# A fused mLSTM cell and gated feed-forward: the head of the kernel is put in another order, and some of its work on other engines

## The chip, the cores and the metric

The kernel runs on one core of a Trainium2 chip. [...] PEld is PE's loading of weights. The metric is the device time of one execution in microseconds.

## The reference

```python
for t in range(S):                      # B=4, H=8, S=768, D=40
    m_new = np.maximum(f_gate[:, :, t] + m, i_gate[:, :, t])
    f_stab = np.exp(f_gate[:, :, t] + m - m_new)
    i_stab = np.exp(i_gate[:, :, t] - m_new)
    m = m_new
    C = f_stab[..., None, None] * C + i_stab[..., None, None] * np.einsum('bhd,bhe->bhde', vt, kt)
    n = f_stab[:, :, None] * n + i_stab[:, :, None] * kt
    h_tilde = np.einsum('bhde,bhe->bhd', C, qt)
    denom = np.maximum(np.abs(np.einsum('bhd,bhd->bh', n, qt)[:, :, None]), 1.0)
    y[:, :, t] = h_tilde / denom / (1.0 + np.exp(-o_gate[:, :, t]))
x = y.transpose(0, 2, 1, 3).reshape(B * S, H * D)     # 3072 x 320
h = x @ w_in                                          # w_in 320 x 2048
out = (h * np.cos(h)) @ w_out                         # w_out 2048 x 320
```

The inputs are fp32; the weights `w_in` and `w_out` are given in fp64.

## The kernel before, in words

The sequence is cut into 6 chunks of 128 steps. One chunk of one batch is a *cell*: 24 cells, n = 0 to 23, 8 heads each. In a cell the recurrence becomes an attention with a decay matrix E (128 x 8 x 128 entries): E comes from the running maxima of the gates, spread over all partitions, less a column of its own (`decay_exponents`), with the upper part cut off by an affine select on GpSimd, and an exponential on ACT (`decay`). Then `turn` (transposes of q and k on PE) and `turn_out` (copies to SBUF), `scores` (q times k), `weigh` (times E), `values` (times v), `normalize` (by the denominators and the sigmoid of `o_gate`, giving y), `seam` (PE turns y into x's layout and makes the state's increment), `seam_out` and `state` (copies from PSUM). For the four cells of the first chunk the state is empty; from cell 4 on (called cell B in the prediction) a carried state is added, and cells are treated in another layout.

When the four cells of a chunk are done, the feed-forward for its 512 tokens can start: 8 pairs of 128-wide blocks of d_ff, each pair an `Up` (products with `w_in` into two PSUM banks, eviction on ACT at `near`, L723, then DVE and ACT make h cos h) and a `down` (products with `w_out`). The next chunk's cells run in between, so the order is: the four cells of chunk 0 (the *head*, `first_cells`, L1063), then for each chunk its feed-forward with the next chunk's cells.

The fp64 weights come as pairs of 32-bit words and are put together on the chip, piece by piece: `take_apart` (two ACT instructions), `bound` (two on DVE), `join` (one on DVE), `round_up` (an integer addition on GpSimd, L187). `weights_in(f)` is three pieces: two of 128x512 and `w_in_l` of 128x256. The raw words land in one of four quarters of the tile `blocks`, used in turn; cell 3's E takes a quarter too.

The order on every engine is written by hand: the program is traced under `tc.manual_schedule()`, and each engine runs its instructions in the order in which the Python code makes them. The code of the head sets it. All loads are issued by SP in one queue, in the code's order; a load that has to wait holds up all behind it. An issue also waits for the load eight places ahead of it.

What the change and the prediction touch:

- Fillings: constant tiles are filled by GpSimd (L101 to L131, L232 to L234) and DVE (L94 to L99, L125) before the head begins.
- `gates_first` (L246): scan, subtraction and scan on DVE for the first chunk's gates; the maxima M0 (32 rows, one for each batch and head) go to DRAM by a DMA of GpSimd (L252), from where they are spread over 128 partitions by a load (`load_M`, L406, 512 KB a cell). For cells in `SPREAD` PE spreads them instead (`spread`, L419: products with a column of the identity repeated 128 times).
- `gates_sums`, `gates_less_sums`, `gates_maxima`, `gates_exponents`, `gates_exp`, `gates_turn`, `gates_diagonal`: the same for the five later chunks, 32 rows of 640. `gates_maxima` ends with a GpSimd DMA to DRAM (L278), which cell B's E is loaded from (L404); `gates_exp` ends with two (L291), which G (L500) is loaded from.
- `warm(k)`: k products of zeros on PE, whose result nobody reads.
- PSUM banks: `psum(n)` gives even cells of the head one pool of two banks and odd ones another of four; the pool of the `Up` has two.

Of the kernel before, what the change touches and what calls it, by code (L numbers as in the profile page):

```python
# [11 lines left out]
FP = mybir.dt.float32  # L12
# [17 lines left out]
def kernel(  # L30
# [33 lines left out]
    NK = DM // 128  # L64
    KL = NK * 128
    assert DM - KL == 64 and NF % 2 == 0
    SPREAD = (0, 1)

    const = ctx.enter_context(tc.tile_pool(name="const", bufs=1))
    wp = ctx.enter_context(tc.tile_pool(name="wp", bufs=1))  # L70
# [9 lines left out]
    ps_o = ctx.enter_context(tc.tile_pool(name="ps_o", bufs=4, space=bass.MemoryType.PSUM))  # L80


    ident = const.tile([128, 128], FP, name="ident")
    make_identity(nc, ident)
    room = const.tile([128, 3, NF // 2, 128], FP, name="room")
    small = room[:, 2].rearrange("p k n -> p (k n)")
    wall = small[:, 0:256].bitcast(BF).rearrange("p (h t) -> p h t", t=C)
    ident_b = small[:, 256:320].bitcast(BF)
    nil = small[:, 320:384].bitcast(BF)
    yo = small[:, 384:384 + DM]  # L90
    blocks = const.tile([128, 40, C], FP, name="blocks")
    S_AT, S_RING, D_AT, D_RING, FREE_AT = 0, 3, 12, 10, 32
    one = const.tile([BH, 1], FP, name="one")
# [1 line left out]
    least = const.tile([128, H], FP, name="least")  # L95
    nc.vector.memset(least, TWO_PI)
    firsts = blocks[:, 32:36]
    M0_all = firsts[:, 2]
    nc.vector.memset(M0_all, 0.0)  # L99

    nc.gpsimd.memset(wall, 0.0)  # L101
    nc.gpsimd.affine_select(out=wall, in_=wall, compare_op=OP.is_ge, fill=1.0e30, base=0,
# [2 lines left out]

    DV = 48
    ks_wide = room[:, 0:2].rearrange("p i k n -> p (i k n)").rearrange("p (b h d) -> p b h d", b=B, h=H)
    nc.gpsimd.memset(ks_wide[:, :, :, D:64], 0.0)
    ks2 = [const.tile([128, 2, H, D], FP, name=f"ks{i}") for i in range(2)]
    vs2 = [const.tile([128, 2, H, DV], FP, name=f"vs{i}") for i in range(2)]  # L110
    for i in range(2):
        nc.gpsimd.memset(vs2[i][:, :, :, D:DV], 1.0)

    vr2 = [const.tile([128, 2, HP, 3, 8, 2], FP, name=f"vr{i}") for i in range(2)]
    for t in vr2:
        nc.gpsimd.memset(t, 1.0)
        nc.gpsimd.memset(t[:, :, :, 1], 0.0)

    WR = HP * (C // 32) * D
    raws = {w: [const.tile([128, WR + 32], FP, name=f"{w}r{i}") for i in range(2)] for w in "qk"}
    for i in range(2):
        for w in "qk":
            nc.vector.memset(raws[w][i], 0.0)  # L125

    st = [const.tile([128, 2 * HP * DV], FP, name=f"st{b}") for b in range(B)]
    for t in st:
        nc.gpsimd.memset(t, 0.0)
    og = const.tile([128, B, 3 * C // 32, 32], FP, name="og")  # L130
    nc.gpsimd.memset(og, 0.0)  # L131

    w_in_sb = wp.tile([128, NK, DFF], FP, name="w_in_sb")

# [94 lines left out]
    a1, F1, M1, keep, shift = (t.rearrange("r (c s) -> r c s", c=R) for t in spare)  # L229
    m0 = gates.tile([BH, R], FP, name="m0")  # L230
    dd = gates.tile([BH, R - 1, BH], FP, name="dd")
    nc.gpsimd.memset(keep, 1.0)  # L232
    nc.gpsimd.memset(keep[:, :, 0:1], 0.0)
    nc.gpsimd.memset(shift, 0.0)  # L234

    fg, ig = (g.rearrange("b h s -> (b h) s") for g in (f_gate, i_gate))

# [8 lines left out]
    def gates_first():  # L246
# [6 lines left out]
        nc.vector.tensor_scalar(out=nM, in0=M0[:, C - 1:C], scalar1=-1.0, scalar2=None, op0=OP.mult)  # L253
        nc.scalar.activation(out=e0, in_=a0, func=AF.Exp, bias=nM)

    def gates_first_out():
        pg = ps_o.tile([128, 2, BH], FP, name="pg", tag="o")
        for j, src in enumerate((a0, e0)):
            nc.tensor.transpose(pg[:, j], src, ident[0:BH, 0:BH])
        nc.vector.tensor_copy(out=tab[:, 0, 0:2], in_=pg)  # L260
# [7 lines left out]
        nc.vector.tensor_tensor_scan(out=flat[0], data0=flat[3], data1=flat[0], initial=0.0, op0=OP.mult, op1=OP.add)  # L268

    def gates_less_sums():  # L270
        nc.vector.tensor_tensor(out=a1, in0=a1, in1=F1, op=OP.subtract)
        nc.vector.tensor_copy(out=shift[:, 0, 0:1], in_=F0[:, last])
        nc.vector.tensor_copy(out=shift[:, 1:R, 0:1], in_=F1[:, 0:R - 1, last])

    def gates_maxima():
        nc.vector.tensor_tensor_scan(out=flat[1], data0=flat[4], data1=flat[2], initial=M0[:, last],
# [106 lines left out]
    def load_E(n):  # L383
        load_M(n)
        if n >= B and n % 2 == 0:
            load_G(n)
# [28 lines left out]
    def spread(n, i):  # L415

        for p in range(HP):
            g = n * H + HP * i + p
            nc.tensor.matmul(pm[n, i][:, p], ident[:, g:g + 1].to_broadcast([128, 128]), M0_all,  # L419
                             start=False, stop=(p == HP - 1))  # L420

    def psum_o():
# [2 lines left out]
    def cols(n, j, width):  # L425
        c, b = divmod(n, B)
        return tab[:, c, j, ts(b, H)].unsqueeze(2).to_broadcast([128, H, width])


    def decay_exponents(n):  # L430
        E = Es[n]
        if n < B:
            nc.vector.tensor_tensor(out=E, in0=E, in1=cols(n, 0, C), op=OP.subtract)
        nc.gpsimd.affine_select(out=E, in_=E, compare_op=OP.is_ge, fill=1.0e30, base=0,  # L434
                                pattern=[[0, H], [1, C]], channel_multiplier=-1)

# [24 lines left out]
    def psum(n):  # L461

        return (ps_o, "o") if n < B and n % 2 == 1 else (ps_a, "a")
# [187 lines left out]

    def seam(n):

        pool, tag = psum(n)
        if n < B:
            px = pool.tile([128, NK + 1, C], FP, name="px", tag=tag)
            for i in range(NK):
                nc.tensor.transpose(px[:, i], ys[n][:, ts(i, 128)], ident)
            for e in range(2):
                nc.tensor.matmul(px[64 * e:64 * e + 64, NK], ys[n][:, KL:DM], ident, start=True, stop=True)  # L660
            pxs[n] = px
        if n < N - B:
            pu = pool.tile([128, HP, DV], FP, name="pu", tag=tag)
            for p in range(HP):
                for j in range(2):
                    h = 2 * p + j
                    nc.tensor.matmul(pu[64 * j:64 * j + D, p], kws[n][:, h], vs(n)[:, h], start=True, stop=True)  # L667
            pus[n] = pu
# [389 lines left out]
    def warm(k, bank=None):  # L1058

        for _ in range(k):  # L1060
            nc.tensor.matmul(bank or pw, nil, nil.unsqueeze(1).to_broadcast([128, HP, 128]), start=True, stop=True)

    def first_cells():  # L1063
        nc.vector.memset(nil, 0.0)
        gates_in()
        nc.scalar.copy(out=ident_b, in_=ident)
        load(0, "qk")
        later_gates_in()
        load(0, "v")
        load(1, "qk")  # L1070
        load_o(0, (0, 1))
        load(1, "v")
        load(2, "qk")
        load_E(0)
        load_E(1)
        warm(12)
        wall_in(0, 0, pmu)
        wall_in(0, 1, psum_o())
        gates_first()
        gates_first_out()  # L1080
        spread(0, 0)
        decay_exponents_half(0, 0)
        turn(0)
        turn_out(0, False)
        gates_sums()
        spread(0, 1)
        decay_exponents_half(0, 1)
        decay(0)
        weigh_k(0)
        load_E(2)  # L1090
        load(2, "v")
        load_E(3)
        load_o(0, (2, 3))
        load(3)
        first = weights_in(0)
        pieces.extend(next(first) for _ in range(NK))
        wall_in(1, 0, psum_o())
        wall_in(1, 1, psum_o())
        gates_less_sums()
        spread(1, 0)  # L1100
        decay_exponents_half(1, 0)
        scores(0)
        gates_maxima()
        turn(1)
        weigh(0)
        sigmoid(0, slice(0, 2))
        turn_out(1, False)
        spread(1, 1)
        decay_exponents_half(1, 1)
        gates_exponents()  # L1110
        decay(1)
        weigh_k(1)
        values(0)
        load_M(B)
        pieces.extend(first)
        load_blocks(B)
        normalize(0)
        scores(1)
        gates_exp()
        load_G_of(B)  # L1120
        turn(2)
        turn_out(2, False)
        gates_turn()
        seam(0)
        load(B, "kv")
        outs.append((0, weights_out(0)))
        load_blocks(B + 1)
        weigh(1)
        seam_out(0)
        state(0)  # L1130
        decay_exponents(2)
        gates_diagonal()
        decay(2)
        weigh_k(2)
        values(1)
        normalize(1)
        scores(2)
        turn(3)
        sigmoid(0, slice(2, 4))
        seam(1)  # L1140
        weigh(2)
        decay_exponents(3)
        turn_out(3)
        seam_out(1)
        values(2)
        decay(3)
        weigh_k(3)
        state(1)
        normalize(2)
        scores(3)  # L1150
        warm(2)
        seam(2)
        weigh(3)
        to_float32(*pieces.pop(0))
        seam_out(2)
        state(2)
        for piece in pieces[0:2]:
            take_apart(*piece)
        values(3)
        pd = gates_spread()  # L1160
        warm(6)
        more = weights_in(1)
        pieces.extend(next(more) for _ in range(NK))
        load_M(B + 1)
        normalize(3)
        bound(pieces[0][0])
        put_together(*pieces.pop(0))
        seam(3)
        seam_out(3)
        decay_exponents(B)  # L1170
        bound(pieces[0][0])
        put_together(*pieces.pop(0))
        gates_keep(pd)
        pieces.extend(more)
        load_G_of(B + 1)
        load(B + 1, "kv")
        outs.append((1, weights_out(1)))
        load_o(1)
        outs.append((2, weights_out(2)))
        low_dimensions(B)  # L1180
        turn_blocks(B)
        state(3)
        decay(B)
        scale_q(B)
        weigh_k(B)
        odd_values_of(B)

    spot = const.tile([1, 1], FP, name="spot")
    nc.gpsimd.memset(spot, 0.0)

    def sin_next():

# [320 lines left out]
```

## Time and profile before

| what | us |
|---|---|
| median of 3 runs | 514.96 (514.72 to 515.9) |
| the profiled execution | 515.31 |
| its span (first to last instruction) | 513.5 |
| PE busy in the span | 498.9 (97%) |
| DVE, ACT, POOL busy | 418.5, 326.4, 301.9 |
| first `values` of cell 0, 1, 2, 3 (PE, L546) | 17.59, 23.89, 28.84, 33.42 |
| first product of the first `Up` (L715) | 38.44 |
| first eviction of the first `Up` (ACT, L723) | 43.77 |

The profile is of one execution. Its rows give a start, a duration, the engine, the line of the kernel, the operation and `out<-in`; in brackets stands how long the engine idled ahead of the row and what ended that. Times in rows are counted from the first instruction.

### The profile page before, as it was taken

What the parts mean: (1) busy time and instruction counts of PE and PEld (TensorE: products, weight loads), DVE (VectorE), ACT (ScalarE), POOL (GpSimd) and SP (SyncE); (2) the same over time, 40 slices, a digit from 0 to 9 for tenths busy, and PEclk for the clock granted to TensorE, in tenths of its full rate; (3) what the DMA queues carried; (4) which work ended last, traced back from release to release, by engine and by line L of the source; (5) the groups of instructions that cost most, each with busy time, mean ns of one, the idle gap of its engine ahead of it and who ended that gap; (6) DMA issues with size and microseconds to landing.
All of it is one profiled execution on the core that took longest, in us unless ns stands there. A gap on an engine that the chain in (4) does not pass through costs nothing.

```text
span 513.5 us, 11097 instructions
## 1 busy us (share of the span) xinstructions
PE 498.9 (97%) x4038; PEld 377.0 (73%) x4038; DVE 418.5 (82%) x839; ACT 326.4 (64%) x618; POOL 301.9 (59%) x387
## 2 busy tenths in 40 slices
PE   6999998999999999999999999999999999999997
PEld 3874554655676677778878778878778878687876
DVE  4889998987788888789988979988979867677655
ACT  2889887686944647748658757658857654443541
POOL 7525656543924955857576868566767455535340
PEclk9999999999999999999999999999999999999999
DMA  9989999899066527306829105928202000010001
GB/s 136 212 187 251 263 194 248 194 257 182 32 173 138 129 73 139 94 32 175 180 65 179 55 31 157 186 76 172 61 32 80 5 5 6 2 52 0 1 0 54
DMA packets 100903, 57.87 MB, mean 113 GB/s; under 512 B 63520, under 2 KB 93312, under 8 KB 100848
## 3 DMA queue, kind: packets, MB, share of 16 engines
q1 hardware_dynamic: 97696, 55.48, 46.3%
q10 hardware_dynamic: 2752, 1.23, 0.9%
q8 instruction: 32, 0.52, 0.5%
q0 software_dynamic: 400, 0.44, 0.3%
q14 instruction: 23, 0.19, 0.1%
HBM read 51.71 MB, written 4.11 MB: 109 GB/s over the span
## 4 chain that ended last, share of the span: by engine, by line
PE 71%; DVE 5%; ACT 5%; DMA 3%; POOL 2%; issue 2%; SPq 1%; ACTq 0%; DVEq 0%; POOLq 0%
PE acc L979 23%; PE pup L783 16%; PE pup L715 7%; PE pup L799 6%; PE late L979 4%; PE po L829 3%; PE ps L530 3%; PE pup L709 2%; PE vt L565 2%; PE vt L556 2%; DVE t L508 1%; DMA bits<-in_moe_w_out_dram 1%; PE pu L667 1%; DMA E<-M_d 1%; ACT E L448 1%
## 5 line engine op out<-in xcount | busy, mean ns | idle before, releaser
L723 ACT ACTIVATE n<-pup 128x512 int32<-128x512 f32 x64 | 36.9, 593 | 96.4 <-DVE pup L808 64.9
L731 ACT ACTIVATE n<-n 128x512 f32<-128x512 f32 x96 | 58.2, 627 | 21.1 <-DVE n L726 15.6
L818 POOL TENSOR_TENSOR g<-g,n 128x512 f32<-128x512 f32 x31 | 39.5, 1275 | 50.9 <-ACT n L731 46.8
L715 PE MATMUL pup<-xT,w_in_sb 128*128 128x512 f32 x128 | 58.8, 602 | 1.9 <-DVE g L735 1.7
L726 DVE SCALAR_TENSOR_TENSOR n<-pup,n 128x512 f32<-128x512 f32 x64 | 43.1, 688 | 21.3 <-ACT n L723 18.8
L979 PE MATMUL acc<-w_out_sb,g 128*128 128x160 f32 x320 | 58.4, 302 | 0.0
L800 POOL TENSOR_TENSOR blocks<-blocks 128x256 f32<-128x256 f32 x32 | 25.6, 801 | 53.3 <-ACT blocks L792 53.2
L979 PE MATMUL acc<-T,g 128*128 128x160 f32 x304 | 55.8, 301 | 0.0
L783 PE MATMUL pup<-xT,w_in_sb 128*128 128x256 f32 x192 | 53.0, 385 | 0.4 <-ACT blocks L792 0.2
L448 ACT ACTIVATE E<-E,tab 128x128 f32<-128x128 f32 x160 | 50.2, 391 | 3.3 <-POOL E L434 3.1
L979 PEld LDWEIGHTS acc<-w_out_sb,g 128*128 128x128 f32 x320 | 48.9, 190 | 4.5 <-issue 2.7
L735 DVE TENSOR_TENSOR g<-pup,n 128x512 f32<-128x512 f32 x64 | 42.6, 687 | 6.0 <-ACT n L731 5.6
L715 PEld LDWEIGHTS pup<-xT,w_in_sb 128*128 128x128 f32 x128 | 23.0, 189 | 33.0 <-issue 31.1
L979 PEld LDWEIGHTS acc<-T,g 128*128 128x128 f32 x304 | 46.0, 190 | 0.9 <-issue 0.4
L783 PEld LDWEIGHTS pup<-xT,w_in_sb 128*128 128x128 f32 x192 | 33.8, 189 | 9.6 <-ACT blocks L792 5.8
L808 DVE TENSOR_TENSOR pup<-pup,blocks 128x256 f32<-128x256 f32 x32 | 13.9, 436 | 30.6 <-PE pup L799 27.3
L783 PE MATMUL pup<-x_room,room 128*128 128x256 f32 x128 | 38.2, 380 | 0.0
L791 ACT COPY blocks<-pup 128x512 f32<-128x512 f32 x32 | 18.6, 580 | 29.8 <-PE pup L783 27.9
L829 PE MATMUL po<-w_out_sb,g 128*128 128x320 f32 x128 | 36.3, 436 | 0.8 <-POOL w_out_sb L187 0.7
L979 PE MATMUL acc<-T,blocks 128*128 128x160 f32 x160 | 36.2, 308 | 0.0
L799 PE MATMUL pup<-xL,w_in_l 64*128 64x512 f32 x128 | 36.1, 641 | 0.0
L512 POOL TENSOR_TENSOR qG<-t,G 128x512 f32<-128x512 f32 x20 | 25.9, 1293 | 17.1 <-DVE t L508 16.8
(214 smaller groups left out, 1221.9 us busy)
## 6 DMA issues: line engine op xcount, KB each, us to landing
E<-M_d SPq DMA_DIRECT2D x21, 512.0 KB
qr<-in_q_dram SPq DMA_DIRECT2D x72, 80.0 KB
kr<-in_k_dram SPq DMA_DIRECT2D x72, 80.0 KB
bits<-in_moe_w_out_dram SPq DMA_DIRECT2D x8, 640.0 KB
G<-G_d SPq DMA_DIRECT2D x18, 256.0 KB
blocks<-in_moe_w_in_dram SPq DMA_DIRECT2D x32, 128.0 KB
out_dram<-o_sb SPq DMA_DIRECT2D x23, 160.0 KB
o<-in_o_gate_dram SPq DMA_DIRECT2D x40, 80.0 KB
```

Source lines behind the costliest of these rows:

```text
L448: nc.scalar.activation(out=Es[n][:, h], in_=Es[n][:, h], func=AF.Exp, scale=-1.0, bias=tab[:, c, 0, g:g + 1])
L512: nc.gpsimd.tensor_tensor(out=qG, in0=qkT[n][0], in1=Gs[n], op=OP.mult)
L715: nc.tensor.matmul(pu.rearrange("p (b t) -> p b t", b=B), w_in_sb[:, i, ts(2 * f2 + e, 128)], xT[c][:, i:NK * B:NK], start=(i == 0 and not ...
L723: nc.scalar.activation(out=self.n[e], in_=self.pu[e], func=AF.Copy, bias=0.25)
L726: nc.vector.scalar_tensor_tensor(out=self.n[e].bitcast(FP), in0=self.pu[e], scalar=0.25, in1=self.n[e], op0=OP.add, op1=OP.subtract)
L731: nc.scalar.activation(out=r, in_=r, func=AF.Sin, scale=TWO_PI_DOWN)
L735: nc.vector.tensor_tensor(out=g, in0=self.pu[e], in1=self.n[e].bitcast(FP), op=OP.mult)
L783: nc.tensor.matmul(bank[:, part].rearrange("p (b t) -> p b t", b=B // 2), w[:, f2], x, start=start, stop=stop, skip_group_check=True)
L799: nc.tensor.matmul(pu, w_in_l[r, f2], xL[c][r].rearrange("p b t -> p (b t)"), start=False, stop=True, skip_group_check=True)
L818: tt(out=self.g, in0=self.g, in1=self.n[e].bitcast(FP), op=OP.mult)
L829: nc.tensor.matmul(po[c][b], gs[c, f][:, ts(b, C)], w_out_sb[:, f], start=(f == 0), stop=(f == NF - 1))
L979: nc.tensor.matmul(a, lhs, rhs, start=start, stop=stop)
```

## The change

The head is put in another order, and some of its work moves to other engines.

- Fillings are done on other engines and at other times: `nil` (zeros for `warm`) first; `ks_wide` on DVE; `raws`, `st`, `vr2` on GpSimd inside the head; only the part of `og` that no load overwrites is zeroed.
- `SPREAD` takes cell 2 in: its E is no longer loaded. The maxima are split into three bf16 parts that add up to the fp32 value (`maxima_in_parts`), stacked in 96 rows of `M0_parts`, and `spread` multiplies them by three stacked identities (`of_parts`) in bf16.
- Loads: cell 3's E and v, q, k follow the second chunk of loads directly, then the first `w_in` pieces, all three ahead of cell B's E.
- `gates_less_sums` and the subtraction of cell 3's E (`decay_exponents`) move from DVE to GpSimd.
- `seam` of the even cells uses the banks of the `Up`.
- `warm` is 9 at the start instead of 12, `warm(2)` goes, `warm(6)` uses another bank. `exp_next` loads ACT's exponential table early.
- The later gates' maxima, exponents and turn come later; the first piece's `put_together` comes after `normalize(3)`.

```diff
-    SPREAD = (0, 1)
+    SPREAD = (0, 1, 2)
...
-    nc.gpsimd.memset(ks_wide[:, :, :, D:64], 0.0)
+    nc.vector.memset(ks_wide[:, :, :, D:64], 0.0)
...
+    def blocks_constants():
+        for i in range(2):
+            for w in "qk":
+                nc.gpsimd.memset(raws[w][i], 0.0)
...
+    def odd_constants():
+        for t in vr2:
+            nc.gpsimd.memset(t, 1.0)
+            nc.gpsimd.memset(t[:, :, :, 1], 0.0)
...
+    def maxima_in_parts():
+
+        rest, mid = blocks[0:BH, 36], blocks[0:BH, 37].bitcast(BF)[:, 0:C]
+        hi = M0_parts[0:BH]
+        nc.vector.tensor_copy(out=hi, in_=M0)
+        nc.vector.tensor_tensor(out=rest, in0=M0, in1=hi, op=OP.subtract)
+        nc.vector.tensor_copy(out=mid, in_=rest)
+        nc.vector.tensor_tensor(out=rest, in0=rest, in1=mid, op=OP.subtract)
+        nc.vector.tensor_copy(out=M0_parts[2 * BH:3 * BH], in_=rest)
+        nc.scalar.copy(out=M0_parts[BH:2 * BH], in_=mid)
...
     def gates_less_sums():
-        nc.vector.tensor_tensor(out=a1, in0=a1, in1=F1, op=OP.subtract)
+        nc.gpsimd.tensor_tensor(out=a1, in0=a1, in1=F1, op=OP.subtract)
...
-            nc.tensor.matmul(pm[n, i][:, p], ident[:, g:g + 1].to_broadcast([128, 128]), M0_all,
+            nc.tensor.matmul(pm[n, i][:, p], of_parts[:, g:g + 1].to_broadcast([128, 128]), M0_parts,
                              start=False, stop=(p == HP - 1))
...
         if n < B:
-            nc.vector.tensor_tensor(out=E, in0=E, in1=cols(n, 0, C), op=OP.subtract)
+            nc.gpsimd.tensor_tensor(out=E, in0=E, in1=cols(n, 0, C), op=OP.subtract)
...
-        pool, tag = psum(n)
+        pool, tag = (ps_u, "up") if n < B and n % 2 == 0 else psum(n)
...
+    def decay_in(n):
+        for i in range(2):
+            wall_in(n, i, pmu if (n, i) == (0, 0) else psum_o())
+        for i in range(2):
+            spread(n, i)
+        for i in range(2):
+            decay_exponents_half(n, i)
```

The end of the new `first_cells`, from cell 2's scores on:

```python
        scores(2)
        weigh(2)
        weigh_k(2)
        seam(1)
        seam_out(1)
        state(1)
        turn(3)
        turn_out(3, False)
        gates_maxima()
        gates_exponents()
        load_M(B)
        load_blocks(B)
        load(B, "kv")
        outs.append((0, weights_out(0)))
        load_blocks(B + 1)
        values(2)
        decay(3)
        sigmoid(0, slice(2, 4))
        scores(3)
        normalize(2)
        weigh(3)
        seam(2)
        weigh_k(3)
        values(3)
        gates_exp()
        load_G_of(B)
        gates_diagonal()
        gates_turn()
        for piece in pieces[0:1]:
            take_apart(*piece)
        bound(pieces[0][0])
        seam_out(2)
        state(2)
        for piece in pieces[1:2]:
            take_apart(*piece)
        pd = gates_spread()
        warm(6, psum_o())
        normalize(3)
        put_together(*pieces.pop(0))
        more = weights_in(1)
        pieces.extend(next(more) for _ in range(NK))
        load_M(B + 1)
        seam(3)
        seam_out(3)
```

## The prediction

> **What bounds the kernel now.** I read the page's tenths first. From the third of the 40 slices on PE is at 9, and from 128 us PE is the whole story. The edits touch only the first 45 us; from the first up projection on, every engine's instructions stand in the old order. So the question is how much earlier or later that projection is reached, and what of the difference survives until PE takes over. The table by stretches shows the head and what follows it (busy us of each engine, granted clock, DMA share, GB/s):
>
> ```profile
> 10.00:20.00 10.00, 9.84 (x93) 9.16 (x94) 7.92 (x14) 6.95 (x9) 3.44 (x6) 1.00 1.10 214
> 20.00:30.00 10.00, 9.71 (x125) 8.66 (x123) 8.17 (x18) 8.98 (x19) 4.64 (x7) 1.00 0.94 205
> 30.00:40.00 10.00, 9.78 (x98) 6.82 (x97) 8.95 (x24) 8.63 (x26) 4.19 (x4) 1.00 0.78 184
> ...
> 44.00:60.00 16.00, 16.00 (x128) 9.02 (x125) 15.20 (x30) 13.46 (x25) 6.65 (x9) 1.00 1.00 242
> 60.00:95.00 35.00, 32.27 (x258) 19.08 (x258) 31.75 (x61) 29.95 (x58) 21.28 (x25) 1.00 0.91 222
> ```
>
> Up to 95 us two things are full: the DMA engines, and from 44 us DVE (15.20 of 16). Nothing there can catch up; a head that ends later leaves its lateness to DVE, and a load that starts later leaves it to the DMAs. The chain of waits shows the one place where they meet:
>
> ```profile
> 50.34 5.67 DMA bits<-in_moe_w_out_dram
> ...
> 56.03 3.38 DMA o<-in_o_gate_dram
> ...
> 59.46 1.28 ACT L352
> ```
>
> There ACT waited 0.68 us for a DMA: compute has 0.68 us to spare against the queue. Next the head's end, by engine and time:
>
> ```profile
> 35.37 1.30 POOL L187 TENSOR_TENSOR w_in_sb<-w_in_sb,blocks 128x512 int32<-128x512 int32 x1 [3.73 <-ACT st L690]
> 38.75 1.41 POOL L187 TENSOR_TENSOR w_in_sb<-w_in_sb,blocks 128x512 int32<-128x512 int32 x1 [2.08 <-DMA vs<-in_v_dram]
> 40.12 1.14 POOL L434 TENSOR_SCALAR_AFFINE_SELECT E<-E 128x1024 f32<-128x1024 f32 x1
> 41.68 0.74 POOL L187 TENSOR_TENSOR w_in_l<-w_in_l,blocks 128x256 int32<-128x256 int32 x1 [0.41 <-issue]
> ```
>
> ```profile
> 38.73 0.28 DVE L173 TENSOR_SCALAR w_in_l<-w_in_l 128x256 f32<-128x256 f32 x1
> 39.05 1.26 DVE L174 TENSOR_SCALAR w_in_l<-w_in_l 128x256 int32<-128x256 int32 x1
> 40.35 1.19 DVE L183 SCALAR_TENSOR_TENSOR w_in_l<-blocks,w_in_l 128x256 int32<-128x256 int32 x1
> ```
>
> The first up projection starts at 38.44, its last products wait for GpSimd's 41.68 row, and its first eviction starts at 43.77 (call this N). Two DVE rows of 0.3 to 0.4 us took 1.26 and 1.19: each ended only as a GpSimd row beside it did. DVE and GpSimd hold each other up when both work on SBUF alone. Rows that read PSUM don't show it (the 128x512 subtraction at 18.06 took 0.67 beside a GpSimd row of 1.26).
>
> ```profile
> M_d<-w_out_sb POOLq DMA_DIRECT2D x1, 80.0 KB, 5.5
> ```
>
> The later maxima reach DRAM 5.5 us after their issue at 17.26; their first load, of cell B's E, is issued at 26.56 and doesn't wait.
>
> **The change, part by part.** Times are the trace's clock; one execution, 515.31 us, a span of 513.5 and 1.8 around it, 0.35 above the median 514.96.
>
> *Fillings.* DVE's four 0.62 us fillings (L125) leave ahead of the gates' scan and 0.72 of `ks_wide` comes (0.74 on GpSimd), with two small ones: the scan starts at about 2.35 instead of 3.88 (the gate's packets end at 2.07). `nil` is filled first, so the warming products start at 1.0 instead of 4.02; nine at 0.425 end at 4.9.
>
> *Maxima in parts.* Five DVE rows of 0.14 to 0.30 (as L253, L249) take 1.1: parts at 4.75, hidden by the warming products. The trace has no such spread in bf16. Below, a bf16 product and its weight load take 0.11 (L1061 at 31.84); above, the fp32 pair takes 0.24. I take 0.11 to 0.13, four in 0.45 against 0.97.
>
> *Early cells.* From there: halves of E at 6.6 (11.37 before), exponential 9.1 (14.06), scores 9.2 (14.35), values of cell 0 at 11.2 (17.59), of cell 1 at 15.5 (23.89). This lead of 6 to 8 us is what the change buys; the rest asks what remains of it.
>
> *DMA.* One broadcast of E (512 KB; 2.5 us at 205 to 214 GB/s) disappears, so cell 3's q, k and v land about 2 us earlier. The fp32 subtraction on DVE (1.21) goes with it.
>
> *Subtraction of cell 3 on GpSimd.* 128x512 takes 1.28 there (L512), so 128x1024 about 2.5. E of cell 3 lands at about 16.2, so it runs 16.2 to 18.7, then the select, 1.1. DVE wants the SBUF-only product of `normalize(0)` at 17.9 and that of `normalize(1)` at 19.4. By the 39.05 row they wait for the GpSimd row at hand: y of cell 0 at 20.4 instead of 18.4, of cell 1 at 22.0 instead of 19.9. Queued behind them on DVE: `weigh(2)` and the scan of the maxima (1.53), which ends at 25.2 (23.6 without the hold-up).
>
> *Late maxima.* They are now written at 25.2, against 17.26. At 5.5 us they land at about 30.5. SP stands at E of cell B, and behind it the blocks, k, v, w_out and the next w_in. Without the wait SP would be there at 26.56 − 2.5 + 2.7 (four w_in_l issues, 26.95 to 29.66, now ahead of it) = 26.8. So 3.7 us are lost to a gain of 2.5; but the 2.1 us that SP waited on E at 31.1 go as well. Net: the queue is between 0.9 us early and 1 us late; I take 0.3 late.
>
> *Sigmoid and exponents.* The second sigmoid moves behind cell 3's exponential on ACT (table load 1.28, 0.74): it ends at 28.5 (26.9 without hold-up) and `normalize(2)` waits for it; y of cell 2 at 30.1, `weigh(3)` to 31.3, values of cell 3 31 to 33. That is 2.4 of the lead left (33.42 before).
>
> *The turn of the gates.* Its ten transposes (0.8) stand on PE behind values of cell 3, its copy (0.41) on ACT ahead of `take_apart` of the first piece (0.67), and on DVE `bound` of that piece (0.92) ahead of `normalize(3)` (1.6): 33.0 + 0.8 + 0.4 + 0.7 + 0.9 + 1.6 = 37.4 for y of cell 3, against 37.09. The lead is gone; without the hold-up it is 35.5.
>
> *Behind y.* Before, GpSimd rounded the first piece at 35.37, under `normalize(3)`. Now `join` (0.69) and rounding (1.30) follow y, so GpSimd has 1.30, 1.14, 1.41 and 0.74 in a row, with DVE's 0.92, 0.69, 0.64 and 0.45 in between, each in the other's way. GpSimd alone: 37.4 + 0.7 + 0.1 + 4.6 = 42.8, low products to 43.9, N at 44.0. With each in turn waiting for the other (0.92 + 0.69 + 0.64 + 0.45 added): N at 46.7. Before, 0.4 of such waiting showed up in GpSimd's rows; I take 60% of the way, N = 45.6.
>
> *Filler for odd values.* 1.1 us on GpSimd ahead of a copy at 44.53, which PE reads at 47.29: 2.5 us of cover, then nothing. *Seams in other banks, sums of the gates, exp_next (1.28 of table load at 14.4):* under the lead, nothing. If the lead were gone by then, the load would cost its 1.28.
>
> Sum: N 1.8 late, of which 0.68 is absorbed where ACT waited: +1.1 us. 515.31 + 1.1 = 516.4, by the median 516.1, so +0.2%. 0.2% (1.0 us) is also about what a measurement here can tell from no change.
>
> [...] The row says 5.5 us for these 80 KB, and the sum stands on it. [...]
>
> **Rivals.**
> *A. Faster.* GpSimd's subtraction doesn't hold DVE up. Place: `normalize(0)` at 17.9. It decides when cell 3's E lands 2.5 us later, after y of cell 1, or when DVE's product goes through beside it. Then y of cell 3 is at 35.5, N at 43.0 (cell B's eight exponentials on ACT end then) to 43.8, the maxima land at 29. Queue and compute are 0.8 to 2.5 early: 512.5 to 514.2, say 513.8. For it: 18.06 went undisturbed, cells lead by 8 us at 16 us. Against it: the y product at 20.61 took 1.09 beside a GpSimd row instead of 0.56.
> *B. Nothing.* N is at most 1.2 late and the 0.68 covers most: 515.0. For it: before, the held-up rows cost GpSimd only 0.4.
> *C. Cold PE.* `warm(2)` is gone, and by my times PE stands from 26.4 to 29.9. Products run at half speed after a pause here: 12 took 5.10 us at the start, 6 took 1.47 at 35.75. Place: values of cell 3 and the transposes, 2.8 us, doubled: 518.9 at the worst. [...]
> [...]
> *D. Queue.* The maxima take 7 us (bigger packets of w_in beside them): E of cell B at 32, everything behind it 1.8 late, and the wait on `o` with it: 516.8.
>
> **How the numbers follow.** Forecast 0.40 (0.33 over 0.2%, 0.07 within), A 0.36 (0.32 faster, 0.04 within), B 0.12 (within), C 0.06 and D 0.06 (slower). Faster 0.32, same 0.23, slower 0.45. The range reaches from A's 512.6 to C's 518.5. The forecast's own is 515.2 (N at 44.5) to 517.6 (46.7 and a late queue).
>
> **What would show it.** Values of cell 0 at about 11 and of cell 1 at 15 to 16; the GpSimd subtraction of about 2.5 us, and the y product beside it longer than 0.56; SP idle 2 to 4 us ahead of cell B's E; ACT waiting for the turned gates and DVE for the first Abs; N after 43.8. Wrong if N is before 43.5, or if E of cell B is issued before 27.

## The result, and the profile after

In the rows PE is TensorE, DVE VectorE, ACT ScalarE and POOL GpSimd; SP is SyncE, which here only issues DMAs. The changed kernel takes 518.73 us (median of five, 517.76 to 518.93); the kernel before, on the same chip, 514.72 (513.95 to 515.9). The ratio is 1.0074, 95% interval 1.0055 to 1.0092: slower by 0.74%, and just above the predicted range. The profiled execution took 518.73, with a span of 516.9 (before 513.5).

| start, us | before | after |
|---|---|---|
| values of cell 0 | 17.59 | 10.61 |
| values of cell 1 | 23.89 | 14.50 |
| values of cell 2 | 28.84 | 22.59 |
| values of cell 3 (and how long they took) | 33.42 (1.98) | 30.20 (3.64) |
| y of cell 3, end | 37.09 | 38.44 |
| first product of the first `Up` | 38.44 | 40.52 |
| first eviction of the first `Up` (N) | 43.77 | 47.32 |

The cells start up to 9.4 us earlier, keep 3.2 of it as far as the values of cell 3, and have lost it all 8 us later. N is 3.55 later and the span 3.4 longer: next to nothing of the lateness was absorbed. The page of after shows in its tenths what was not there before, in the row of the granted clock: the third slice (25.8 to 38.8 us) has 5, half speed.

```profile
span 516.9 us, 11081 instructions
...
PE   9978998999999999999999999999999999999997
...
PEclk9959999999999999999999999999999999999999
```

A fine table of the clock puts the fall at 26.87 and the rise at 40.53: 13.65 us. Here is the table by stretches of 3.41 us, a quarter of that, around it (busy us of PE, PEld, DVE, ACT, POOL, then granted clock, DMA share, GB/s):

```profile
23.46:26.87 3.41, 2.10 (x26) 1.86 (x24) 0.74 (x5) 3.36 (x5) 2.99 (x5) 1.00 0.93 236
26.87:30.28 3.41, 1.97 (x23) 1.52 (x23) 2.88 (x6) 2.51 (x3) 2.21 (x4) 0.50 0.49 138
30.28:33.70 3.42, 3.42 (x16) 3.41 (x16) 0.00 (x0) 0.00 (x0) 0.00 (x0) 0.50 1.12 262
33.70:37.11 3.41, 3.41 (x17) 2.14 (x17) 0.95 (x4) 2.04 (x7) 0.00 (x0) 0.50 0.94 266
37.11:40.52 3.41, 3.12 (x26) 1.59 (x24) 2.19 (x8) 2.55 (x9) 1.34 (x2) 0.50 1.07 248
40.52:43.93 3.41, 1.98 (x4) 0.67 (x4) 3.31 (x5) 3.25 (x13) 2.27 (x2) 1.00 0.80 220
```

From 30.28 to 33.70 PE works alone, at half speed, while DVE, ACT and GpSimd stand: the chain runs through PE's cold products. The rows of that stretch, PE first, then who waits:

```profile
28.32 0.69 PE L680 MATMUL px<-ident,y 128*128 128x128 f32 x2 [2.75 <-DVE y L646]
...
30.20 3.64 PE L568 MATMUL ph<-vs,blocks 128*128 128x41 f32 x16
33.77 1.27 PE L324 MATMUL pg<-ident,w_out_sb 32*128 32x32 f32 x10
```

```profile
35.08 0.43 ACT L325 COPY tab<-pg 128x320 f32<-128x320 f32 x1 [5.68 <-PE pg L324]
```

```profile
36.09 0.43 DVE L182 TENSOR_SCALAR w_in_sb<-w_in_sb 128x512 f32<-128x512 f32 x1 [6.30 <-ACT w_in_sb L176]
```

PE had stood for 2.75 us ahead of the transposes of cell 2, waiting for y (in the kernel before, `warm(2)` stood there). ACT waits 5.68 for the turn of the gates, DVE 6.30 for the first piece, and only then comes `normalize(3)`, and after it N:

```profile
47.32 1.09 ACT L745 ACTIVATE n<-pup 128x512 int32<-128x512 f32 x2 [1.82 <-PE pup L731]
```

This is rival C, to which the prediction gave 0.06.

### The profile page after: what moved, and what is told of

Its sections match the earlier page's. It is cut to its first block, busy times and chain, and to the rows that moved or that the text cites. A ratio compares the mean times of both kernels' runs of the same rounds, so it can differ in the third digit from the quotient of the medians.

```text
span 516.9 us, 11081 instructions
## 1 busy us (share of the span) xinstructions
PE 500.5 (97%) x4027; PEld 377.8 (73%) x4027; DVE 417.3 (81%) x838; ACT 327.7 (63%) x624; POOL 305.6 (59%) x393
## 4 chain that ended last, share of the span: by engine, by line
PE 67%; DMA 10%; DVE 7%; SPq 5%; issue 4%; POOL 4%; ACT 3%; DVEq 0%; POOLq 0%; ACTq 0%
PE acc L1001 21%; PE pup L805 15%; PE pup L737 6%; PE pup L821 6%; PE late L1001 4%; PE ps L552 3%; DMA G<-G_d 3%; PE po L851 3%; DMA bits<-in_moe_w_out_dram 2%; DMA qr<-in_q_dram 2%; PE pup L731 2%; DMA blocks<-in_moe_w_in_dram 2%; PE vt L587 2%; PE vt L578 1%; DVE n L748 1%
```

## The experiments

Times are medians; the ratio is to the kernel before on the same chip. "Wide products" are those of `warm`: 128x512 in bf16, of zeros, whose result nobody reads. "With the clock up" means: over the executions alone whose mean granted clock is 0.998 or more, as 3.41 us at half speed, the shortest fall in the traces of the head, takes 0.0033 off the mean (3.41 x 0.5 / 515). N is read in the profiled execution.

### Wide products in PE's pause, and the subtraction back on DVE

Theories: *the clock*; *the hold-up* of DVE's y product by GpSimd's subtraction; *the queue*, that is, the late maxima that SP waits for.

```diff
         weigh(3)
+        warm(10, psum_o())
         seam(2)
```

> The changed kernel with ten empty bf16 products on PE ahead of the transposes of cell 2, where PE stood from 25.6 to 28.3 us. They need 2.2 us, and the y they would otherwise wait for ends at 28.4. The clock theory (the granted clock fell at 26.9 because PE stood, and stayed at 0.50 until 40.5): the clock stays at 1.00; the values of cell 3 take 2.0 us instead of 3.64, the turn of the gates 0.75 instead of 1.27, and y of cell 3 ends at 36.1 instead of 38.44; the first eviction of the first up projection (47.32) comes at 44.5 to 45.0, the time at 515.7 to 516.5 us. The queue theory (the late maxima stand in SP's way, and the loads behind them set the pace): values of cell 3 faster all the same, but the first eviction at 46.5 or later and the time at 517.8 or more. The hold-up theory (GpSimd's subtraction costs DVE about 2 us, the clock the rest): 517.0 to 517.5.

516.43 us, ratio 1.0028 (1.0013 to 1.0042); N 45.01.

```profile
28.92 1.98 PE L568 MATMUL ph<-vs,blocks 128*128 128x41 f32 x16
...
35.05 0.41 PE L680 MATMUL px<-ident,y 128*128 128x128 f32 x2 [1.72 <-DVE y L646]
...
37.12 6.80 PE L737 MATMUL pup<-xT,w_in_sb 128*128 128x512 f32 x8 [0.95 <-POOL w_in_sb L196]
```

The values of cell 3 are back at 1.98, and more than half of the loss is gone, as the clock theory said. But the clock still falls, later: PE stood 1.72 us ahead of cell 3's transposes, the clock was at half speed from 36.31 to 43.13, and the first `Up` took 6.80 us, where it had taken 3.75 in the kernel before.

```diff
-            nc.gpsimd.tensor_tensor(out=E, in0=E, in1=cols(n, 0, C), op=OP.subtract)
+            nc.vector.tensor_tensor(out=E, in0=E, in1=cols(n, 0, C), op=OP.subtract)
```

> The changed kernel with cell 3's subtraction on DVE again (128x1024 in 1.2 us) instead of GpSimd (1.90 us). Hold-up theory: y of cell 1 ends 1.5 to 2 us earlier than 20.9, everything behind it as well, and the time is 516.5 to 517.2. Clock theory: y of cell 1 ends at 20.3, 0.6 earlier, because DVE now does the subtraction itself; PE still stands for more than 2 us before the transposes of cell 2, the clock falls again, and the time is 517.8 to 518.7.

518.69, ratio 1.0053 (1.0036 to 1.0070); N 47.30, against 47.32. PE stood 2.75 us again and the clock fell for 10.24 us. The place of the subtraction alone is worth nothing that shows: what GpSimd cost DVE by the hold-up, DVE now pays by doing it.

Both edits together:

> The changed kernel with both edits: the ten empty products in PE's pause and cell 3's subtraction on DVE. Clock theory: what the products alone give (515.7 to 516.5), less 0.3 to 0.7. Hold-up theory: 514.5 to 515.2, as the two costs add up. Queue theory: 517.5 or more.

516.40, ratio 1.0015 (1.0002 to 1.0028); N 45.51, the first `Up` cold again (6.88). The two costs don't add up: the hold-up theory, in the size that the prediction gave it, falls. The 0.3 to 0.7 us that the clock theory expected below the products alone (516.43) didn't come either.

### The kernel before without its two products

```diff
-        warm(2)
         seam(2)
```

> The kernel before without the two empty products ahead of cell 2's transposes (31.84 us). If the fall of the clock comes from the pause and not from the two products that are missing, nothing changes: PE stands for 0.5 us there at most, the clock stays at 1.00, and the time is 514.2 to 515.2. If the two products alone kept the clock up, the clock falls to 0.50 for a stretch between 32 and 45 us, and the time is 516.5 to 518.5.

515.25, ratio 0.9999 (0.9986 to 1.0012); PE stands 0.42 us there and the clock stays at 1.00. Two products missing are nothing in the old order. It is the new order that makes a pause of 2.75 us in their place: the second sigmoid, which y of cell 2 needs, comes behind cell 3's exponential on ACT.

### Both pauses filled, and then the order and the maxima

```diff
-        warm(6, psum_o())
+        warm(14, psum_o())
```

(besides the ten)

> The changed kernel with ten empty products ahead of cell 2's transposes and fourteen instead of six ahead of cell 3's, where PE stood from 33.3 to 35.05 us in the run with ten alone (there the clock fell at 36.4 and stayed at 0.50 until 43.1, over the first up projection). Clock theory: the clock stays at 1.00 through the head; the first up projection's eight products take 3.75 us or wait for GpSimd only, its low products start when GpSimd's last rounding ends, at 42.2, and the first eviction comes at 43.3 to 43.7 (45.01 with ten alone, 43.77 before); the time is 514.2 to 515.2 us. Queue theory: the loads behind E of cell B set the pace; the eviction comes earlier but the time stays at 516 or more.

515.94, ratio 1.0020 (1.0002 to 1.0037). Eight of its twelve executions have the clock up, and lie at 515.18 to 516.28, median 515.60; the kernel before, on the same chip and with the clock up, lies at 514.72. So with the clock up the change costs 0.9 us, where the changed kernel as it is costs 3.6 to 4.0 (518.50 against 514.91 on one chip, 518.73 against 514.72 on another). The expected 514.2 to 515.2 was 0.4 too low for these executions, and 0.7 for the median. The profiled execution was one of the four others, and shows a long hold-up that by itself made PE stand, so the eight may also be those with less of it, and 0.9 a little too low:

```profile
17.26 2.72 DVE L646 TENSOR_TENSOR y<-room,dn 128x256 f32<-128x256 f32 x2
```

```profile
16.77 1.90 POOL L455 TENSOR_TENSOR blocks<-blocks,tab 128x1024 f32<-128x1024 f32 x1 [2.30 <-DMA blocks<-M_d]
18.74 1.16 POOL L456 TENSOR_SCALAR_AFFINE_SELECT blocks<-blocks 128x1024 f32<-128x1024 f32 x1
```

Here E of cell 3 landed 0.9 us earlier than in the first trace, and GpSimd started before y of cell 0 and not behind it. The two instructions of y ended with the two GpSimd rows (19.98 and 19.90) instead of after 0.56; PE stood, the clock fell at 20.3 already, and N was 46.81.

The same with the first piece in its old place:

```diff
+        to_float32(*pieces.pop(0))
         gates_turn()
-        for piece in pieces[0:1]:
-            take_apart(*piece)
-        bound(pieces[0][0])
...
         normalize(3)
-        put_together(*pieces.pop(0))
```

> The same, and the first piece of w_in is taken apart, bounded, joined and rounded ahead of the turn of the gates and of cell 3's division, as in the kernel before. If the place of the first piece behind y of cell 3 costs what the prediction said (the turn's copy, the piece's 0.7 on ACT and 0.9 on DVE stand in the way of y, and four GpSimd rows follow it): y of cell 3 ends at 33 instead of 35.05, the first eviction comes 1.5 to 2 us earlier than with the products alone (41.3 to 42.2), and the time falls by 1 to 2 us if the loads allow it, to 513 to 514. If the loads bind: same eviction gain, and less than 0.5 us of it in the time.

515.38, ratio 1.0015 (0.9998 to 1.0033); with the clock up 514.61 (six executions), 1.0 below the fourteen and ten products alone. y of cell 3 ended at 34.54, not 33: its product took 1.83, held up by GpSimd's rounding. N 43.13, as the fourteen products kept PE until 35.57, past y. The median misses the expected 513 to 514. The order is the second cost, of about 1 us in the time. With both pauses filled and this order, 514.61 stands against 514.72 of the kernel before, both with the clock up: the two costs together account for the loss.

The same as the ten and fourteen products, with the late maxima early:

```diff
         normalize(0)
+        gates_maxima()
         turn(2)
...
         turn_out(3, False)
-        gates_maxima()
         gates_exponents()
```

> The changed kernel with the ten and fourteen products, and the scan of the later maxima (1.53 us on DVE) with its transfer moved up behind cell 0's division. The transfer is issued at about 19.9 instead of 23.7 and lands at 24 to 25, so SP issues E of cell B at 26.5 to 27 instead of 28.8. Queue theory: the time is 1.5 to 2 us under that with the products alone. Compute theory: within 0.4 us of it, as the loads are not what the head's end waits for; y of cell 1 is up to 1 us later.

519.55, ratio 1.0090 (1.0060 to 1.0121): 3.6 us worse than without it. E of cell B was issued at 27.12, earlier than in the changed kernel (28.19), so the queue got what it wanted, and the time went the other way. Only one execution kept its clock, at 517.33. The scan moved y of cell 1 into GpSimd's rows:

```profile
19.93 3.25 DVE L646 TENSOR_TENSOR y<-room,dn 128x256 f32<-128x256 f32 x2
```

PE stood 2.52 us for it, and the clock fell at 24.33. By itself this is no clean test of the queue, as the edit also moved y. The traces taken together are: in the sixteen of the changed kernel and its versions N lies anywhere from 41.74 to 50.79, with E of cell B issued anywhere from 26.40 to 28.76, and the eviction that starts at 109.5 us in the kernel before is each time as late or early as N is, to within 0.35 us. What sets the pace lies ahead of N, and the queue theory is out.

> All three edits. If the first piece's place and the late maxima are costs of two paths that meet behind the head, this gains more than the sum of each alone: 512.3 to 513.3 us. If only compute binds: as with the order alone, 513 to 514.

517.74, ratio 1.0072 (1.0042 to 1.0103): all three are worse than two, for the same reason.

That order alone, with no products added:

> The changed kernel with the first piece of w_in put together ahead of the turn of the gates and of cell 3's division, and no products added: the clock can fall as it does in the changed kernel. Theory of one cause (the clock alone makes the head late): the values of cell 3 still take 3.6 us and end at 33.8, so the first eviction comes at 46 or later and the time is 517.5 or more. Theory of two causes that lie on one path (cold products, and the turn of the gates with the first piece behind them ahead of y): y of cell 3 no longer waits for the turn's copy, ends at 35.4 to 36 instead of 38.44, GpSimd's first rounding is done under the cold products, and the first eviction comes at 44.5 to 45.5 instead of 47.32; the time is 515.5 to 516.7 us.

517.34, ratio 1.0063 (1.0039 to 1.0088); N 45.48.

```profile
29.52 3.64 PE L568 MATMUL ph<-vs,blocks 128*128 128x41 f32 x16
```

```profile
34.19 0.56 DVE L646 TENSOR_TENSOR y<-room,dn 128x256 f32<-128x256 f32 x2
```

The values are as cold as in the changed kernel, yet y of cell 3 ends at 34.75 instead of 38.44 and N is 1.8 earlier than there (45.48 against 47.32). So both causes lie on one path, as the second theory said; the time was 0.6 above its range.

### What the clock follows

```diff
+    def narrow(k, bank):
+        for _ in range(k):
+            nc.tensor.matmul(bank[:, 0, 0:32], nil, nil[:, 0:32], start=True, stop=True)
...
         weigh(3)
+        narrow(44, psum_o())
         seam(2)
```

> The changed kernel with PE's pause ahead of cell 2's transposes filled by 44 narrow bf16 products (128x32, each with a weight load) instead of ten of 128x512. If the granted clock follows whether PE is busy, these hold it up as the wide ones did: values of cell 3 in 1.98 us, and 515.7 to 516.8 us. If it follows how many columns are streamed (in the changed kernel PE was busy without a gap from 28.9 to 38.3 and the clock still stayed at 0.50 until 40.5, and most of those products stream 41 or 128 columns), the clock falls all the same at 26 to 29, values of cell 3 take 3.6 us, and the time is 518 to 519.

518.27, ratio 1.0061 (1.0045 to 1.0078). The 44 took 1.26 us, PE stood 1.00 behind them, the clock fell at 28.95 and the values of cell 3 took 3.58. As a pause was left, the same with 80 of them:

```diff
-        narrow(44, psum_o())
+        narrow(80, psum_o())
```

> The changed kernel with 80 narrow bf16 products (128x32) in PE's pause ahead of cell 2's transposes, where 44 filled only 1.26 of its 2.3 us. PE then stands there for 0.5 us at most, as with ten wide products. If the clock follows busy time, it stays up over the values of cell 3 as it did with the wide ones (1.98 us) and the time is 515.7 to 516.8 us. If it follows the columns streamed, it falls all the same between 26 and 30 us, the values of cell 3 take 3.5 us or more, and the time is 517.8 to 519.

516.62, ratio 1.0034 (1.0016 to 1.0052), with mean clocks from 0.992 to 1.000, three of twelve with the clock up. By the median the 80 do as well as the ten wide ones (1.0028). In the profiled one (515.56) the 80 took 2.17, PE stood 0.66, and the clock stayed at 1.00, also behind a pause of 1.72 ahead of cell 3's transposes, as long as the one that let it fall with the ten wide ones:

```profile
29.25 1.98 PE L568 MATMUL ph<-vs,blocks 128*128 128x41 f32 x16
...
44.19 1.09 ACT L745 ACTIVATE n<-pup 128x512 int32<-128x512 f32 x2 [2.28 <-PE pup L731]
```

So the clock stayed up with 80 narrow products in the pause, against the theory of streamed columns as it was put. This trace also gives the price of the fall, as the edit only fills the pause: y of cell 3 ends at 35.37 and not at 38.44, and N is 44.19 and not 47.32, 3.1 us earlier both times (0.15 of it is there at the end of y of cell 2). But busy time does not settle what holds the clock up either, as the last version but one will show.

### Versions that mend the costs

Ten products, the first piece in its old place, and nine products instead of fourteen:

```diff
-        warm(14, psum_o())
+        warm(9, psum_o())
```

> The ten wide products, the first piece ahead of the turn, and nine instead of fourteen products ahead of cell 3's transposes, which then start when y is there (34.5) and not at 35.57. The first eviction comes 0.7 to 1.1 us ahead of the 43.13 with fourteen, if compute binds; the time is 513.3 to 514.5. If the nine let the clock fall, the first up projection runs cold and the time is 515 to 516.

514.92, ratio 1.0000 (0.9983 to 1.0017); N 41.74, two us ahead of the kernel before, of which 1.3 are left in the time of this execution (514.00 against 515.31):

```profile
41.74 1.09 ACT L745 ACTIVATE n<-pup 128x512 int32<-128x512 f32 x2 [1.03 <-PE pup L731]
```

With the clock up it takes 514.26 (six executions, 512.95 to 515.06). So compute did bind, and a lead can be carried through in good part; the expected 513.3 to 514.5 holds for these executions, the median is missed. Next, cell 3's maxima on PE as well:

```diff
-    SPREAD = (0, 1, 2)
+    SPREAD = (0, 1, 2, 3)
...
-        decay_exponents(3)
+        decay_in(3)
```

> The same as the run before it in this call, and cell 3's maxima are spread on PE as bf16 parts as well, so its E (512 KB) isn't loaded and GpSimd neither subtracts nor selects for it; DVE takes the two 128x512 halves from PSUM (1.28 us). Hold-up theory (GpSimd's subtraction lengthens y of cell 0 or of cell 1 by 1.6 to 2.2 us, depending on when E of cell 3 lands): both y products take 0.56, y of cell 1 ends 0.5 to 1 us earlier, the slower executions with a late y of cell 0 go, and the median is 0.5 to 1 us lower, 512.8 to 514. Otherwise within 0.4 us of the run before it.

514.97, ratio 1.0001 (0.9986 to 1.0017). With the clock up again 514.25, but its six executions lie within 514.05 to 514.40, where the run before had 512.95 to 515.06: without GpSimd's rows in y's way (both y products took 0.56) there is less scatter, and the median stays where the hold-up theory expected 0.5 to 1 us less, as PE and DVE now do the work (N 42.44). Then cell 3's share behind `normalize(1)`, its exponential ahead of cell 1's copies on ACT, and eight products instead of ten in the first pause:

```diff
         normalize(1)
+        decay_in(3)
+        decay(3)
         scores(2)
...
         values(2)
-        decay(3)
         sigmoid(0, slice(2, 4))
```

> A version without the costs found so far: cell 3's maxima spread on PE, behind cell 1's division, so that neither GpSimd nor a transfer is in their way; its exponential ahead of cell 1's copies on ACT, where ACT stood for 1.8 us, so that the sigmoid starts about 1 us earlier; eight and nine wide products in PE's pauses; the first piece of w_in ahead of the turn. Both y products of cells 0 and 1 take 0.56, y of cell 2 ends at about 27.2 (28.2 with GpSimd's subtraction), the first eviction comes at 40.7 to 41.5 (43.77 in the kernel before), and with the clock up the time is 512.5 to 513.5 us, below both kernels; the median, with the executions where the clock falls for a window or two, 513 to 514. If the loads behind the late maxima bind by then, the eviction comes so early and the time stays at 514 to 515.

513.62, ratio 0.9983 (0.9965 to 1.0001); with the clock up 513.48 (eight of twelve), against 514.71 of the kernel before. The median is within the expected 513 to 514. The interval reaches 1, as the clock still falls in a third of the executions. The profiled execution is one of the other four: y of cell 1 took 1.09 where 0.56 was expected, N was 42.82, and the clock fell at 31.43. The 3.41 us ahead of that:

```profile
28.02:31.43 3.41, 3.41 (x47) 3.30 (x48) 3.27 (x10) 1.76 (x4) 1.52 (x3) 1.00 0.95 271
```

PE was busy for all of it, and PEld for 3.30: transposes, the increment, the values, the turn. All are short products with a weight load each. So a busy PE row was no guard here. Last, the wide products spread over the stretch:

```diff
+        fill = psum_o()
+        warm(4, fill)
         scores(3)
...
         weigh(3)
-        warm(8, psum_o())
+        warm(5, fill)
...
         values(3)
+        warm(4, psum_o())
...
-        warm(9, psum_o())
+        warm(6, psum_o())
```

> The version that joins the mended costs, with its wide products spread: four ahead of cell 3's scores, five behind them, four ahead of the turn of the gates and six behind it (eight and nine in two heaps before). In the profiled run with two heaps the clock fell at 31.4 for 3.4 us although PE had not stood for more than 0.22 us since 28.0; between 27.2 and 31.8 it had no wide product. If long products are what holds the clock up, no execution or one falls now where four of twelve did, and the median is 513.0 to 513.6. If not, the share of executions that fall stays, and the median is 513.4 to 514.2.

514.30, ratio 0.9986 (0.9976 to 0.9996): faster than the kernel before by 0.14%, with an interval that ends just below 1. Both expected medians (513.0 to 513.6, and 513.4 to 514.2) are missed. Eleven of twelve executions have the clock up, within 514.12 to 514.61; in the twelfth, the profiled one, it fell at about 220 us, not in the head, where N came at 42.06. One fall in twelve against four in twelve is a difference of few executions. On the same chip the changed kernel, unedited:

> The changed kernel again, unedited, on the same chip as the run before it in this call. By the clock theory every execution has the clock at half speed for three windows of 3.4 us or more (a mean clock of 0.990 or less), and 518 to 519 us; the version with the mended costs stands 4.5 to 6 us below it.

518.50, ratio 1.0072 (1.0049 to 1.0095), mean clocks 0.979 to 0.990: an estimated 10.3 us or more at half speed in every execution (0.010 x 515 / 0.5), and 4.2 us more than the version above (4.5 to 6 expected). In the profiled one the fall came at 30.47 and the rise at 44.12, and y of cell 0 was the one held up (2.26).

## Why the prediction was wrong, step by step

**The direction was right, the size not.** The step that failed is the one that isn't in the sum: PE's pause between the scores of cell 3 and the transposes of cell 2 was costed at nothing, and stood among the rivals as C. C had its place and size right (values and transposes doubled, 2.8 us, "518.9 at the worst"; measured 3.1 us of N, and 518.73) and its chance, 0.06, too low. By the prediction's times PE would stand 3.5 us; it stood 2.75, and the clock fell 1.3 us into the pause. How long a pause it takes, no run shows. With the clock up the changed kernel costs 0.9 us (the two pauses filled), and the sum had said 1.1. That is in part luck: in the trace with the clock up (the 80 narrow products) y of cell 3 ends at 35.37, not 37.4, and N is 44.19, 0.4 late and not 1.8. Nor did the signs by which the prediction would have shown itself wrong (N before 43.5, E of cell B before 27) look at the clock; neither came.

- *Fillings, maxima in parts, early cells:* right. Scan at 2.56 (2.35 said), values at 10.61 and 14.50 (11.2, 15.5). The first two rows of four bf16 spreads took 0.52 and 0.39 (0.45 said), a later row of eight 0.61.
- *Subtraction on GpSimd:* the mechanism was right, the size too large. It took 1.90, not 2.5, and started at 17.70, not 16.2, so y of cell 0 slipped through (0.56) and only y of cell 1 was held up:

```profile
18.68 2.22 DVE L646 TENSOR_TENSOR y<-room,dn 128x256 f32<-128x256 f32 x2
```

  It ended at 20.90, not 22.0. In other executions y of cell 0 was caught (2.72, 2.26). Rival A put all its weight on this step; taking the subtraction off GpSimd gave nothing, as DVE then did it (518.69).
- *Late maxima:* the scan ended at 23.55 (25.2 said), the transfer took 4.18 (5.5), and SP issued E of cell B at 28.19 (30.5). SP lost 1.4 us, not 3.7, and the pace was set elsewhere (the sixteen traces above). Rival D, which needed 7 us for the transfer, is out.
- *Sigmoid:* ended at 26.72 (28.5); it does hold y of cell 2, and makes PE's pause.
- *Turn of the gates and behind y:* the chain was right, link by link, but the prediction let it begin too late: y of cell 2 ended at 28.40 (30.1 said). With the clock up (the 80 narrow products) y of cell 3 ends at 35.37 and N is 44.19, so 8.8 us lie between them where 8.2 were said (37.4 to 45.6). The first piece's old place takes 1.0 us off the time.
- *Absorption of 0.68:* it came and was lost again. Just behind that wait, the third pair of evictions (65.9 us in the kernel before) is 2.88 late, the fourth (74.7) 3.54 again, and from the fifth on they are 3.2 late. The 0.3 that remains appears also where N is early, so it isn't lateness absorbed.

What makes the clock fall was not shown; the traces give this. The falls lasted 13.65 us (the changed kernel), 10.24 (the subtraction back on DVE), 6.83 (ten wide products) and 3.41 (the last version but one), and they begin at another time in each execution (26.87 and 30.47 for the changed kernel). PE's standing alone doesn't tell them: PE was busy 2.10 of the 3.41 us ahead of the first fall, and 3.41 of 3.41 ahead of the one at 31.43. Nor did a stretch with PE busy for 3.42 (30.28 to 33.70) bring the clock back. And in the run with the subtraction back on DVE the clock stayed up with PE busy for 1.73:

```profile
41.92:45.33 3.41, 1.73 (x5) 0.63 (x4) 3.31 (x6) 3.07 (x12) 1.70 (x2) 1.00 0.88 272
```

With short fp32 products with a weight load each (the values: 16 in 1.98 us) the clock fell at 31.43; with 44 narrow ones in the first pause (1.26 us) it fell at 28.95, and with 80 (2.17 us, 27 ns each) or ten wide ones it stayed up over the values of cell 3. Yet in the kernel before without its two products, short ones alone ran from 19.8 to 35 us with no pause over 0.42, and the clock stayed at 1.00. The last version has wide products in the place where the one before it lost its clock, and eleven of its twelve executions have the clock up; that its spread products work by this is argued, not shown.

## What to carry to other kernels

When a change pulls work forward, look for the new pauses of PE, and read the granted clock behind each, not only how long the pause is: here it fell in one of 2.75 us, fell behind one of 1.72 in one run and stayed up behind one of 1.72 in another, and fell once with PE busy for all of the 3.41 us ahead. Price the products behind it at half speed for 3.41 to 13.65 us, as long as these falls lasted. Wide products that nobody reads were cheap there (ten took the ratio from 1.0074 to 1.0028), if they end before the awaited operand comes (fourteen kept PE until 35.57, past y at 34.54) and stand, as far as the few executions tell, in several heaps rather than one (one fall in twelve executions against four). Look, too, where a large GpSimd row comes to lie beside a short DVE row that works on SBUF alone: here such a row took 2.22 to 3.25 us where it met two GpSimd rows (1.90 and 1.16), and its usual 0.56 where it ended as the first of them began (17.71 and 17.70), so a landing time that moves by a microsecond (0.9 here) turns into scatter.

## What the runs showed of the hardware that was not expected

- The granted clock fell with PE busy for the whole 3.41 us ahead of it, and stayed at 0.50 through 3.42 us of busy PE. The busy row and the weight-load row were almost equal there (3.41 and 3.30, 3.42 and 3.41).
- The time at half speed was 3.41, 6.83, 10.24 or 13.65 us in the traces of the head, and its start moved from execution to execution (26.87 and 30.47 for one kernel). In the last version but one eight executions with the clock up lie within 0.7 us, the four others 1.3 to 3.2 us above their median.
- A DVE row of two SBUF-only instructions that met two GpSimd rows ended with the second of them: 2.72 and 3.25 us for 0.56 of work.
